# Beside the MLP, attention steps taken in twos: the order of one core's instructions rewritten for one stage of an attention-then-MLP kernel

## The chip, the core and the metric

The kernel runs on one core of a Trainium2 chip. A core has a matrix engine (PE, whose weight loads are shown as PEld), a vector engine (DVE), a scalar engine (ACT), a general engine (POOL) and a queue engine (SP) that issues most DMAs. Each takes its instructions in its own order and waits for the others through semaphores. Matrix products land in PSUM, eight banks of 128 x 512 float32. The metric is the device time of one execution in microseconds, lower is better.

## What is computed

```python
# q, k, v: 8 batches x 8 heads x 576 rows x 64; omega: 128 x 64
def phi(x):
    proj = np.einsum('bhsd,md->bhsm', x, omega)
    sq = np.sum(x * x, axis=-1, keepdims=True) / 2.0
    h = proj - sq
    h = h - np.max(h, axis=-1, keepdims=True)
    return np.exp(h) / np.sqrt(m)
q_p, k_p = (phi(q_s), phi(k_s))              # q_s, k_s: q and k scaled
kv = np.einsum('bhsm,bhsd->bhmd', k_p, v)
z = np.sum(k_p, axis=2)
num = np.einsum('bhsm,bhmd->bhsd', q_p, kv)
den = np.einsum('bhsm,bhm->bhs', q_p, z)[..., None] + 1e-06
x = (num / den)                              # then reshaped to 4608 x 512
g = x @ w_gate                               # 512 x 1536
out = (g * (1.0 / (1.0 + np.exp(-g))) * (x @ w_val)) @ w_out
```

All in float32. The MLP's products are made of three matmuls each, from a high and a low part of both operands (`hi`, `lo`).

## The kernel before

Attention works on groups of 256 rows of two heads: 72 groups of queries and 72 of keys. A step holds two groups: two of keys in the first six steps, then one of queries and one of keys, and two of queries in the last six (72 steps in all). A step goes through these functions, and they are what the order is made of:

- `st_transpose`: four PE transposes of the loaded rows (`nat`) into a bank `pt`, copied by ACT to `x`; POOL squares `nat` into `sq`.
- `st_project`: matmuls of `x` with `omT` into two banks `pp`. Each uses 64 of the array's 128 rows, and two run side by side. The profile shows 16 records for them, since a float32 matmul has two records.
- `st_max` (DVE: row sums of `sq`, maxima of both `pp`) and `st_exp` (ACT: eight exponentials from `pp` into `ph`).
- `k_accumulate`: matmuls of a key group's `ph` with `v` into the bank `kvacc`, two steps later. When a pair of heads is complete, `kv_finalize` copies `kvacc` to `kvr`, and for batches from 4 on transposes the row of sums (`zp`), copies it and sends it through DRAM (`zd`), from where `load_z` spreads it over all partitions (`zt`).
- the output of a query group in one of two ways. For batches 0 to 3: `q_transpose` (four transposes into `ptq`, copied by ACT to `qt`), `q_mult` (matmuls with `kvr` into `po`, divided on DVE into `xn`), then `q_out`, which transposes `xn` into `xt`. For batches 4 to 7 the divisor is made first (`q_den`: POOL product `jk`, DVE sum and reciprocal `dj`; `q_norm`: POOL scales `ph`), then `q_transpose`, and `q_out` multiplies `kvr` with `qt`, which gives the output already turned (`xt`, with 64 output columns per matmul). ACT then copies `xt` to `xo`, which is sent to DRAM for the last stage, or to `xh`, with DVE making `xl`.

PSUM is dealt out in pools: three banks for the MLP (`ps_moe`), two for projections (`ps_proj`), one bank `ps_att`, one bank `ps_tr`, and one for `kvacc`.

The kernel has three stages. Up to step 24 attention runs nearly alone (`CLOSE`). From step 25 (`EARLY`) on each step is one turn of the list `GROUPED`: its functions in turn, and between them six entries `SHARE`, at which the MLP stream is given its part of the work (`give`) and the conversion of the weights a few operations (`tick`). The MLP stream works through three tiles of 512 rows; per visit of a tile it makes three `g`, four `o` of the visit before, three `v`. When attention is done, the pools of attention are released, `first_x` prepares the operands of the last stage on DVE and ACT beside the last MLP work, and the last stage computes six tiles in pairs with seven products (`a`, `c`, `d`) in place of eight. It is not touched.

The order in the program is the order in which the functions are called, but a scheduler of the language may move an instruction ahead of others on its engine where its operands are there.

Of the kernel before, what the change touches and what calls it, by code (L numbers as in the profile page):

```python
# [24 lines left out]
def kernel(  # L25
# [16 lines left out]
    P = 128  # L42
# [387 lines left out]
    def st_transpose(n):  # L430
        if n >= NS:
            return
        nat = nats.pop(n)
        pt = ps_tr(f"pt_{n}", [P, 2, G])
        for i in range(2):
            for c in range(CH):
                turned_in[:] = [
                    transpose(
                        pt[:, i, c * P : (c + 1) * P], nat[:, i, c].rearrange("p h d -> p (h d)"), ident
                    )  # L440
                ]
        x = att.tile([P, 2, G], F32, name=f"x_{n}", tag="x")

        st = att.tile([P, 4, 2, CH, 2], F32, name=f"st_{n}", tag="st", bufs=6)
        sq = att.tile([P, 2, CH, 2, D], F32, name=f"sq_{n}", tag="sq")
        nc.gpsimd.tensor_tensor(sq, nat, nat, op=ALU.mult)  # L446
        if 3 <= n < EARLY:
            nc.scalar.copy(x[:, 0], pt[:, 0])
            nc.vector.tensor_copy(x[:, 1], pt[:, 1])
            for w in (D // 2, D // 4):  # L450
                lower_, upper_ = (sq[..., o : o + w].rearrange("p i c h d -> p (i c h) d") for o in (0, w))
                nc.gpsimd.tensor_tensor(lower_, lower_, upper_, op=ALU.add)
        else:
            nc.scalar.copy(x, pt)  # L454
        sts[n] = x, st, sq
        return True

    def st_project(n):
        if n >= NS:
            return  # L460
        x, st, sq = sts[n]

        new = ps_moe if n < EARLY and n % 2 else ps_proj
        pp = [new(f"pp{hh}_{n}", [P, 2, CH, M]) for hh in range(2)]
        for i in range(2):
            for c in range(CH):
# [51 lines left out]
    def kv_finalize(b, a2):  # L518
        acc = kvacc.pop((b, a2))
        raw = att.tile([P, 4, VW], F32, name=f"kvr{b}_{a2}", tag="kvr", bufs=4)  # L520
        nc.scalar.copy(raw, acc)  # L521
        for j in range(2):
            kvst[b, 2 * a2 + j] = raw[:, 2 * j : 2 * j + 2, :]
        if b >= BPOOL:

            zp = ps_att(f"zp{b}_{a2}", [4, P])
            transpose(zp, raw[:, :, D], ident)
            zs = att.tile([4, P], F32, name=f"zs{b}_{a2}", tag="zs")
# [5 lines left out]
    zds = {}  # L534
    zbc = {}

    def load_z(n):
# [12 lines left out]
    def q_den(n):  # L550

        n -= JLAG
        for _, b, g, gr in slots(n, "q"):
# [10 lines left out]
            else:  # L564
# [5 lines left out]
            dn = att.tile([P, 3, CH, 2], F32, name=f"dj{b}_{g}", tag="dj", bufs=6)  # L570
# [64 lines left out]
    def q_mult(n):  # L635

        n -= MLAG
        for _, b, g, gr in slots(n, "q"):
            if b >= BPOOL:
                continue  # L640
            qt = qts.pop((b, g))
            po = ps_att(f"po{b}_{g}", [P, CH, 2, VW])
            for c in range(CH):
                prs = pairs_of(gr)[c]
                w = P // len(prs) if gr is None else P
# [11 lines left out]
            xn = att.tile([P, CH, 2, D], F32, name=f"xn{b}_{g}", tag="jx")  # L657
            nc.vector.tensor_tensor(
                xn.rearrange("p c h d -> p (c h) d"),
                po[:, :, :, 0:D].rearrange("p c h d -> p (c h) d"),  # L660
# [10 lines left out]
    cols_done = [0]  # L671

    def q_out(n):
        n -= OLAG
        for i, b, g, gr in slots(n, "q"):
            po = (ps_att if n + OLAG < EARLY or i else ps_tr)(f"xt{b}_{g}", [P, G])
            first = column(b, gr)
            if b < BPOOL:
                xn = xns.pop((b, g))
                for c in range(CH):  # L680
                    transpose(po[:, c * P : (c + 1) * P], xn[:, c].rearrange("p h d -> p (h d)"), ident)
            else:
                qt = qts.pop((b, g))

                segs = [(pr, pr * RES, RES) for pr in range(NPAIR)] if gr is None else [(gr[0], 0, G)]
                for pr, o, w in segs:
                    for hh in range(2):
                        matmul(
                            po[hh * D : (hh + 1) * D, o : o + w], kvst[b, pr][:, hh, 0:D], qt[:, hh, o : o + w],
                            start=True, stop=True, skip_group_check=True,  # L690
                        )
            j, o = tile_of(first)
            if gr is None:
                parts_ = [(po.rearrange("d (r c) -> d r c", c=RES), slice(0, NPAIR), j, o, RES)]
# [18 lines left out]
        return bool(slots(n, "q"))  # L713


    def mm1(ps, wts, xs):
# [403 lines left out]
    def turn_next(n):  # L1120
# [11 lines left out]
        lambda n: k_accumulate(n, 1),  # L1132
        st_exp,
        q_den,
        lambda n: n == EARLY - 1 and q_out(n),
        lambda n: n == EARLY - 1 and q_mult(n),
    )
    GROUPED = (
        q_out,
        st_project,  # L1140
        q_transpose,
        lambda n: k_accumulate(n, 0),
        lambda n: k_accumulate(n, 1),
        st_max,
        st_exp,
        q_den,
        lambda n: st_transpose(n + 1),
        SHARE,
        SHARE,
        SHARE,  # L1150
        lambda n: q_norm(n + 1),
        q_mult,
        SHARE,
        SHARE,
        SHARE,
    )

    for n in range(2):
# [8 lines left out]
    warm(2, turned_in[0])  # L1167
    loaded = 3
    ends = []
    for n in range(NN):  # L1170
        if loaded <= n + LA:
            load(loaded)
            loaded += 1
# [3 lines left out]
            loaded += 1  # L1177
        if n == FIRST_RAW:
            load_raw(0)
        want = OPS * np.interp(clock[n + 1], [clock[m] for m, _ in marks], [x for _, x in marks])  # L1180
        order = CLOSE if n < EARLY else GROUPED
        left = len(order) if n < EARLY else order.count(SHARE)
        for what in order:
            with ExitStack() as es:
                if n < EARLY:
                    for ins in ends if what is st_project else ends[:1]:
                        es.enter_context(tc.issue_after(ins.ins))
                if what is not SHARE:
                    what(n)
            if n < EARLY:  # L1190
                if what is st_project:
                    ends.clear()
                ends.append(newest_pe[0])
            if what is turn_next and n < 2:
                warm(2, turned_in[0])
            if n < EARLY or what is SHARE:
                due = course[n + 1] - given[0] - debt[0]
                if due > 0:
                    give(due / left)
                for _ in range(int(np.ceil((want - ticks[0]) / left))):  # L1200
                    tick()
                left -= 1
        load_z(n)
    late.close()
    for name, pool in (
        ("win", tc.tile_pool(name="win", bufs=1)),
# [38 lines left out]
```

## Time and profile before

| | us |
|---|---|
| median of 3 runs | 1166.98 (1164.1 to 1167.11) |
| the profiled execution | 1166.82 |
| its span, first to last instruction | 1165.0 |
| first MLP matmul starts | 111 |
| last `xt` of attention starts | 562.7 |
| first product `a` of the last stage starts | 610.9 |

The profile is of one execution, so sums are made against 1166.82. Rows of groups give a line, an engine, the operation, tiles written and read, the shape, a count, the busy time and the mean of one in ns, then idle time ahead of it and what ended it. Rows in order of time give start, length, engine, line, operation and count; idle time ahead stands in brackets. Rows of stages give the stretch, its length, busy time and number of instructions of PE, PEld, DVE, ACT and POOL, the granted clock of PE, the DMA share and GB/s.

### The profile page before, as it was taken

Reading aid. Unit: us, or ns where it says so; the run is one execution under the profiler, and the core shown is the slowest. Engines: PE = TensorE matmul, PEld = TensorE weight load, DVE = VectorE, ACT = ScalarE, POOL = GpSimd, SP = SyncE. Lnnn points to the kernel's source line nnn. Section 1 sums busy time; section 2 is a strip of 40 time slices with the busy share of each in tenths; the row PEclk is TensorE's granted clock in tenths of the full one; section 3 lists DMA queues with packets and bytes.
Section 4 is the critical chain, followed back from the end, with each engine's and each line's share of the span. In section 5 each row is a group of like instructions: output and inputs, shape, how many; then the busy total and the mean of one; then the engine's idle time right before and its main releaser. Section 6 shows DMA issues by size and latency. Waiting matters only on the chain.

```text
span 1165.0 us, 18915 instructions
## 1 busy us (share of the span) xinstructions
PE 1137.2 (98%) x6645; PEld 939.5 (81%) x6646; DVE 707.4 (61%) x1289; ACT 678.3 (58%) x1539; POOL 615.5 (53%) x559
## 2 busy tenths in 40 slices
PE   8999999999999999989999999999999999999998
PEld 6888888888878778867788778888878888888886
DVE  5787667455656656565474566665566666456654
ACT  5887886876776866757434544454544445444441
POOL 5664433344556675587245555544455543455551
PEclk9999999999999999999999999999999999999999
DMA  6764445655445642322544111124211111211103
GB/s 137 179 160 114 128 142 161 178 135 143 122 126 137 168 132 78 114 68 65 154 118 126 46 55 55 55 74 122 59 55 55 54 37 46 81 55 55 46 19 72
DMA packets 173966, 114.30 MB, mean 98 GB/s; under 512 B 125840, under 2 KB 144304, under 8 KB 173872
## 3 DMA queue, kind: packets, MB, share of 16 engines
q1 hardware_dynamic: 172528, 112.78, 35.5%
q8 instruction: 52, 0.85, 0.3%
q10 hardware_dynamic: 1344, 0.33, 0.1%
q14 instruction: 42, 0.34, 0.1%
HBM read 87.88 MB, written 25.18 MB: 97 GB/s over the span
## 4 chain that ended last, share of the span: by engine, by line
PE 74%; DVE 10%; ACT 6%; POOL 4%; DMA 3%; issue 2%; SPq 1%; ACTq 0%; POOLq 0%; DVEq 0%
PE o L103 22%; PE a L103 16%; PE c L103 8%; PE g L103 6%; PE pp L103 4%; PE v L103 4%; PE d L103 4%; PE kvacc L103 3%; ACT ph L505 3%; PE ptq L107 2%; PE po L103 2%; PE pt L107 2%; PE xt L103 1%; DVE st L490 1%; POOL wlo L264 1%
## 5 line engine op out<-in xcount | busy, mean ns | idle before, releaser
L505 ACT ACTIVATE ph<-pp,st 128x128 f32<-128x128 f32 x576 | 157.8, 386 | 26.5 <-DVE st L493 26.0
L763 DVE TENSOR_TENSOR acc<-o,acc 128x512 f32<-128x512 f32 x156 | 105.8, 684 | 94.6 <-PE o L103 94.3
L446 POOL TENSOR_TENSOR sq<-nat 128x512 f32<-128x512 f32 x72 | 78.2, 1086 | 130.5 <-DVE st L483 89.1
L950 POOL TENSOR_TENSOR wlo<-wspare,whi 128x512 fp32r<-128x512 f32 (+1 forms) x60 | 61.0, 1037 | 117.4 <-ACT whi L949 111.0
L490 DVE TENSOR_REDUCE st<-pp 128x4 f32<-128x512 f32 x144 | 92.5, 683 | 39.0 <-PE pp L103 38.7
L264 POOL TENSOR_TENSOR wlo<-wraw,whi 128x512 fp32r<-128x512 f32 x59 | 82.7, 1406 | 26.7 <-ACT whi L263 22.8
L103 PE MATMUL pp<-omT,x 64*128 64x128 f32 x1152 | 87.3, 285 | 3.2 <-ACT x L454 2.2
L103 PEld LDWEIGHTS pp<-omT,x 64*128 64x128 f32 x1152 | 72.6, 187 | 20.2 <-issue 11.2
L950 POOL TENSOR_TENSOR wlo<-s,whi 128x512 fp32r<-128x512 f32 x64 | 82.6, 1311 | 3.8 <-ACT whi L949 3.8
L1059 ACT COPY late<-a 128x512 f32<-128x512 f32 x72 | 42.2, 586 | 59.7 <-PE a L103 58.5
L103 PE MATMUL o<-whi,late 128*128 128x512 f32 x192 | 74.5, 389 | 0.0
L571 DVE TENSOR_REDUCE dj<-jk 128x4 f32<-128x512 f32 x36 | 24.6, 684 | 73.5 <-POOL jk L567 60.6
L103 PE MATMUL kvacc<-v,ph 128*128 128x65 f32 x512 | 65.9, 268 | 0.5 <-ACT kvr L521 0.5
L824 POOL TENSOR_TENSOR hl<-sl,hh 128x512 fp32r<-128x512 f32 x36 | 47.0, 1308 | 34.8 <-ACT hh L823 34.7
L103 PEld LDWEIGHTS kvacc<-v,ph 128*128 128x128 f32 x512 | 63.1, 192 | 0.8 <-ACT kvr L521 0.6
L1063 DVE TENSOR_TENSOR late<-c,late 128x512 f32<-128x512 f32 x25 | 17.3, 692 | 69.7 <-PE c L103 60.6
L103 PE MATMUL g<-xh,whi 128*128 128x512 f32 x144 | 59.4, 412 | 0.0
L103 PE MATMUL o<-whi,hh 128*128 128x512 f32 x144 | 58.5, 406 | 0.1
L303 POOL TENSOR_TENSOR wc<-st 128x512 int32<-128x512 int32 x36 | 37.5, 1042 | 39.6 <-DVE st L298 17.2
L103 PE MATMUL v<-xh,whi 128*128 128x512 f32 x144 | 57.9, 402 | 0.0
L103 PE MATMUL g<-xh,wlo 128*128 128x512 f32 x144 | 57.7, 401 | 0.0
L103 PE MATMUL g<-xl,whi 128*128 128x512 f32 x144 | 57.2, 397 | 0.0
(261 smaller groups left out, 3369.4 us busy)
## 6 DMA issues: line engine op xcount, KB each, us to landing
wraw<-wscr SPq DMA_DIRECT2D x63, 256.0 KB, 2.7
wspare<-wscr SPq DMA_DIRECT2D x60, 256.0 KB, 2.8
wscr<-wc SPq DMA_DIRECT2D x36, 256.0 KB, 2.2
out_dram<-acc SPq DMA_DIRECT2D x72, 128.0 KB, 2.4
nat<-in_k_dram SPq DMA_DIRECT2D x64, 128.0 KB, 3.0
nat<-in_q_dram SPq DMA_DIRECT2D x64, 128.0 KB, 3.1
v<-in_v_dram SPq DMA_DIRECT2D x62, 128.0 KB, 3.5
st<-in_moe_w_gate_dram SPq DMA_DIRECT2D x12, 512.0 KB, 4.1
```

Of the source, the lines that this page charges most:

```text
L103: newest_pe[:] = [nc.tensor.matmul(*args, **kw)]
L107: newest_pe[:] = [nc.tensor.transpose(*args, **kw)]
L264: nc.gpsimd.tensor_tensor(lo, raw, hi.bitcast(F32), op=ALU.subtract)
L303: nc.gpsimd.tensor_tensor(ui, ri, low, op=ALU.add)
L446: nc.gpsimd.tensor_tensor(sq, nat, nat, op=ALU.mult)
L490: nc.vector.tensor_reduce(st[:, 1, :, :, hh], pp[hh], axis=AX.X, op=ALU.max, negate=True)
L505: step_end["s"] = nc.scalar.activation(ph[:, c, hh * M : (hh + 1) * M], pp[hh][:, i, c, :], AF.Exp, bias=st[:, 3, i, c, hh : hh + 1], scal ...
L571: nc.vector.tensor_reduce(dn[:, 0], jk, axis=AX.X, op=ALU.add)
L763: nc.vector.tensor_tensor(a_, po, a_, op=ALU.add)
L824: nc.gpsimd.tensor_tensor(hl, h, hh.bitcast(F32), op=ALU.subtract)
L950: nc.gpsimd.tensor_tensor(lo, src_, hi.bitcast(F32), op=ALU.subtract)
L1059: newest["s"] = nc.scalar.copy(keep[name], ps)
```

## The change

From step 25 on, one turn of a new list `DOUBLE` does two steps, n and n + 1 (24 turns with projections). Each entry names a function and which of the two steps it is for.

```diff
-        new = ps_moe if n < EARLY and n % 2 else ps_proj
-        pp = [new(f"pp{hh}_{n}", [P, 2, CH, M]) for hh in range(2)]
+        if n < EARLY:
+            new = (ps_moe, ps_moe) if n % 2 else (ps_proj, ps_proj)
+        else:
+            new = (ps_proj, ps_proj) if (n - EARLY) % 2 else (ps_att, ps_tr)
+        pp = [new[hh](f"pp{hh}_{n}", [P, 2, CH, M]) for hh in range(2)]
...
         if b >= BPOOL:
-            zp = ps_att(f"zp{b}_{a2}", [4, P])
+            zraw[b, a2] = raw
+    def z_rows():
+        for (b, a2), raw in zraw.items():
+            zp = ps_moe(f"zp{b}_{a2}", [4, P])
             transpose(zp, raw[:, :, D], ident)
...
-            po = ps_att(f"po{b}_{g}", [P, CH, 2, VW])
+            odd = n + MLAG >= EARLY and (n + MLAG - EARLY) % 2
+            po = (ps_tr if odd else ps_att)(f"po{b}_{g}", [P, CH, 2, VW])
...
+    def q_out_both(n):
+        groups = slots(n - 1 - OLAG, "q") + slots(n - OLAG, "q")
+        at = []
+        for k_, g_ in enumerate(groups):
+            if k_ % 2 == 0:
+                two = ps_moe(f"xt{g_[1]}_{g_[2]}", [P, 2, G])
+            at.append((g_, two[:, k_ % 2]))
+        place_out(at)
...
-    GROUPED = (
-        q_out,
-        st_project,
-        q_transpose,
-        lambda n: k_accumulate(n, 0),
-        lambda n: k_accumulate(n, 1),
-        st_max,
-        st_exp,
-        q_den,
-        lambda n: st_transpose(n + 1),
-        SHARE,
-        SHARE,
-        SHARE,
-        lambda n: q_norm(n + 1),
-        q_mult,
-        SHARE,
-        SHARE,
-        SHARE,
+    DOUBLE = (
+        (lambda n: k_accumulate(n, 0), 0),
+        (q_out_both, 0),
+        (st_project, 0),
+        (st_project, 1),
+        (lambda n: k_accumulate(n, 1), 0),
+        (q_norm, 0),
+        (st_max, 0),
+        (st_exp, 0),
+        (q_den, 0),
+        (st_max, 1),
+        SHARE,
+        SHARE,
+        SHARE,
+        (q_norm, 1),
+        SHARE,
+        SHARE,
+        SHARE,
+        (lambda n: z_rows(), 0),
+        (load_z, 0),
+        (load_z, 1),
+        (lambda n: k_accumulate(n, 0), 1),
+        (q_transpose, 0),
+        (st_transpose, 2),
+        (st_exp, 1),
+        SHARE,
+        SHARE,
+        (q_transpose, 1),
+        (st_transpose, 3),
+        (lambda n: k_accumulate(n, 1), 1),
+        SHARE,
+        SHARE,
+        (q_mult, 0),
+        (q_mult, 1),
+        SHARE,
+        SHARE,
+        (q_den, 1),
     )
...
+    for n in range(EARLY, NN, 2):
+        loads(n)
+        loads(n + 1)
+        left = DOUBLE.count(SHARE)
+        last = min(n + 2, NN)
+        for what in DOUBLE:
+            if what is not SHARE:
+                what[0](n + what[1])
+                continue
+            share(course[last] - given[0] - debt[0], wanted(last), left)
+            left -= 1
```

`place_out` is the body of the old `q_out`: it writes all groups' `xt` first and copies them afterwards. The buffers of `st` and `dj` go from six to four, `zs` from two to one, and `xn` gets a tag of its own, since it no longer fits beside `jk`'s. The last step of `CLOSE` no longer makes the output of step 24 and transposes the inputs of step 26 in place of it.

Three places on the engines' queues, as the programs hold them (the names are the tiles of the list above; `pp0_47` is step 47's projection of the first head).

PE, steps 47 and 48, the stretch with the projections. Before, step 47 alone; the matmuls left out are six more of `pp`, and MLP work follows the last row:

```order
L103 MATMUL xt4_2_4308<-qt4_2_4236,kvr4_1_3569 64x256 x2
L103 MATMUL pp0_47_4314<-omT_96,x_47_4268 128x128
L103 MATMUL pp1_47_4315<-omT_96,x_47_4268 128x128
...
L107 MATMUL ptq4_3_4324<-ident_90,ph0_45_4137 128x128 x4
L103 MATMUL kvacc5_1_4127<-v5_102,ph1_45_4142 128x65 x4
L107 MATMUL pt_48_4356<-ident_90,nat48_4088 128x128 x4
```

After, with six more of `pp` left out twice, between MLP matmuls on both sides:

```order
L103 MATMUL kvacc5_1_4126<-v5_102,ph1_45_4142 128x65 x2
L103 MATMUL xt4_1_4306<-qt4_1_4221,kvr4_0_3078 64x256 x2
L103 MATMUL xt4_1_4306<-qt4_2_4249,kvr4_1_3603 64x256 x2
L103 MATMUL pp0_47_4317<-omT_96,x_47_4228 128x128
L103 MATMUL pp1_47_4318<-omT_96,x_47_4228 128x128
...
L103 MATMUL pp0_48_4327<-omT_96,x_48_4256 128x128
L103 MATMUL pp1_48_4328<-omT_96,x_48_4256 128x128
...
L103 MATMUL kvacc5_1_4126<-v5_102,ph1_45_4142 128x65 x2
```

The two steps' outputs and projections stand in one stretch, and the transposes have left it. Counted over PE's order from step 25 to the last `xt`, stretches of `xt` matmuls and `pp` without other work between them go from 55 to 33, and stretches of MLP matmuls from 84 to 78.

ACT in the same turn, from the exponentials of step 47 to the copies of the second transposing group (`hh` is the MLP's, `st8` and `wc8` are the conversion's):

```order
L508 ACTIVATE ph1_47_4350<-pp1_47_4318,st_47_4229 128x128 x2
L301 ACTIVATE st8_0_3988<-st8_0_3988 128x512
L289 ACTIVATE wc8_1_4389<-st8_1_4191 128x512
L845 CAST hh4_4_4395<-sl4_4_4160 128x512
L643 COPY qt4_3_4420<-ptq4_3_4415 128x512
L454 COPY x_49_4427<-pt_49_4422 128x512
L508 ACTIVATE ph0_48_4432<-pp0_48_4327,st_48_4257 128x128 x2
```

Before, the same engine there (step 47's exponentials, then step 48's):

```order
L505 ACTIVATE ph1_47_4345<-pp1_47_4315,st_47_4269 128x128 x2
L301 ACTIVATE st8_0_4068<-st8_0_4068 128x512
L289 ACTIVATE wc8_1_4389<-st8_1_4196 128x512
L823 CAST hh4_4_4394<-sl4_4_4165 128x512
L703 COPY xo4_3_4_4418<-xt4_3_4415 128x256
L823 CAST hh4_5_4476<-sl4_5_4167 128x512
L633 COPY qt4_4_4436<-ptq4_4_4431 128x512
L454 COPY x_49_4468<-pt_49_4463 128x512
```

The copies of the transposes now stand between the exponentials of a pair's first and second step. On PE the transposes that they copy stand like this in the turn of steps 47 and 48; an MLP tile `g` follows:

```order
L107 MATMUL ptq4_3_4415<-ident_90,ph0_45_4137 128x128 x4
L107 MATMUL pt_49_4422<-ident_90,nat49_4085 128x128 x4
L103 MATMUL kvacc5_1_4126<-v6_103,ph1_46_4238 128x65 x2
L107 MATMUL ptq4_4_4443<-ident_90,ph0_46_4233 128x128 x4
L107 MATMUL pt_50_4450<-ident_90,nat50_4293 128x128 x4
```

In ten turns the two halves of this group stand together like this or with one or two MLP matmuls between them; in the others an MLP tile of 9 or 12 matmuls stands there. Between the projections and the first `ptq` stand 18 to 30 MLP matmuls, in five turns 12.

PE around the row of sums of batch 5 (`zp5_1`). Before, behind the accumulation that completes it:

```order
L107 MATMUL ptq4_5_4531<-ident_90,ph0_47_4340 128x128 x4
L103 MATMUL kvacc5_1_4127<-v7_104,ph1_47_4345 128x65 x4
L107 MATMUL pt_50_4571<-ident_90,nat50_4301 128x128 x4
L107 MATMUL zp5_1_4544<-ident_90,kvr5_1_4542 4x128
L103 MATMUL g5_5_4589<-xh2_1706,whi5_0_3210 128x512
```

After, where `kvacc5_1` was completed 12 MLP matmuls ahead of these rows:

```order
L103 MATMUL g5_5_4582<-xh2_1706,wlo5_0_3317 128x512
L107 MATMUL zp5_1_4598<-ident_90,kvr5_1_4545 4x128
L103 MATMUL kvacc6_0_4604<-v0_97,ph1_48_4437 128x65 x2
L107 MATMUL ptq4_5_4607<-ident_90,ph0_47_4345 128x128 x4
L107 MATMUL pt_51_4614<-ident_90,nat51_4300 128x128 x4
```

Behind the last `xt` of attention, 204 MLP matmuls stood ahead of the first product `a` of the last stage, and 180 stand there now.

More of the change, by code (lines that the diff above doesn't have):

```diff
@@ L442, in st_transpose @@
         x = att.tile([P, 2, G], F32, name=f"x_{n}", tag="x")
-        st = att.tile([P, 4, 2, CH, 2], F32, name=f"st_{n}", tag="st", bufs=6)
+        st = att.tile([P, 4, 2, CH, 2], F32, name=f"st_{n}", tag="st", bufs=4)
         sq = att.tile([P, 2, CH, 2, D], F32, name=f"sq_{n}", tag="sq")
@@ L524, in kv_finalize @@
         if b >= BPOOL:
-            zp = ps_att(f"zp{b}_{a2}", [4, P])
+            zraw[b, a2] = raw
+    zraw = {}
+    zds = {}
+    def z_rows():
+        for (b, a2), raw in zraw.items():
+            zp = ps_moe(f"zp{b}_{a2}", [4, P])
             transpose(zp, raw[:, :, D], ident)
-            zs = att.tile([4, P], F32, name=f"zs{b}_{a2}", tag="zs")
+            zs = att.tile([4, P], F32, name=f"zs{b}_{a2}", tag="zs", bufs=1)
             nc.scalar.copy(zs, zp)
@@ L532, in kv_finalize @@
             zds[b, a2] = zd
-    zds = {}
+        zraw.clear()
     zbc = {}
@@ L569, in q_den @@
                 )
-            dn = att.tile([P, 3, CH, 2], F32, name=f"dj{b}_{g}", tag="dj", bufs=6)
+            dn = att.tile([P, 3, CH, 2], F32, name=f"dj{b}_{g}", tag="dj", bufs=4)
             nc.vector.tensor_reduce(dn[:, 0], jk, axis=AX.X, op=ALU.add)
@@ L656, in q_mult @@
             nc.vector.reciprocal(dn[:, 1], dn[:, 0])
-            xn = att.tile([P, CH, 2, D], F32, name=f"xn{b}_{g}", tag="jx")
+            xn = att.tile([P, CH, 2, D], F32, name=f"xn{b}_{g}", tag="xn")
             nc.vector.tensor_tensor(
@@ L673, in q_out, with place_out @@
     def q_out(n):
-        n -= OLAG
-        for i, b, g, gr in slots(n, "q"):
-            po = (ps_att if n + OLAG < EARLY or i else ps_tr)(f"xt{b}_{g}", [P, G])
+        place_out([(g_, (ps_att if n < EARLY else ps_tr)(f"xt{g_[1]}_{g_[2]}", [P, G])) for g_ in slots(n - OLAG, "q")])
+    def q_out_both(n):
[6 more added lines that the diff above has]
+        place_out(at)
+    def place_out(at):
+        for (i, b, g, gr), po in at:
             first = column(b, gr)
@@ L691, in q_out @@
                         )
+        for (i, b, g, gr), po in at:
+            first = column(b, gr)
             j, o = tile_of(first)
@@ L712, in q_out @@
                 cols_done[0] = first + (RES if gr is None else G)
-        return bool(slots(n, "q"))
     def mm1(ps, wts, xs):
@@ L1134 @@
         q_den,
-        lambda n: n == EARLY - 1 and q_out(n),
         lambda n: n == EARLY - 1 and q_mult(n),
+        lambda n: n == EARLY - 1 and st_transpose(n + 2),
     )
-    GROUPED = (
-        q_out,
-        st_project,
-        q_transpose,
-        lambda n: k_accumulate(n, 0),
-        lambda n: k_accumulate(n, 1),
-        st_max,
-        st_exp,
-        q_den,
-        lambda n: st_transpose(n + 1),
+    DOUBLE = (
[9 more added lines that the diff above has]
+        (st_max, 1),
         SHARE,
@@ L1169, with loads @@
     ends = []
-    for n in range(NN):
+    def loads(n):
+        nonlocal loaded
         if loaded <= n + LA:
@@ L1179, with share, wanted @@
             load_raw(0)
[L1180 to L1183, printed above, removed]
-            with ExitStack() as es:
[L1185 to L1193, printed above, removed]
+    def share(due, want, left):
+        if due > 0:
+            give(due / left)
+        for _ in range(int(np.ceil((want - ticks[0]) / left))):
+            tick()
+    def wanted(n):
+        return OPS * np.interp(clock[n], [clock[m] for m, _ in marks], [x for _, x in marks])
+    for n in range(EARLY):
+        loads(n)
+        for at, what in enumerate(CLOSE):
+            with ExitStack() as es:
+                for ins in ends if what is st_project else ends[:1]:
+                    es.enter_context(tc.issue_after(ins.ins))
+                what(n)
+            if what is st_project:
+                ends.clear()
+            ends.append(newest_pe[0])
             if what is turn_next and n < 2:
                 warm(2, turned_in[0])
[L1196 to L1202, printed above, removed]
-        load_z(n)
+            share(course[n + 1] - given[0] - debt[0], wanted(n + 1), len(CLOSE) - at)
+        load_z(n)
+    for n in range(EARLY, NN, 2):
+        loads(n)
+        loads(n + 1)
[7 more added lines that the diff above has]
+            left -= 1
     late.close()
```

## The prediction

> **What bounds the kernel now.** I read the page first, then the sums by stage, then the waits of PE alone.
>
> ```profile
> span 1165.0 us, 18915 instructions
> PE 1137.2 (98%) x6645; PEld 939.5 (81%) x6646; DVE 707.4 (61%) x1289; ACT 678.3 (58%) x1539; POOL 615.5 (53%) x559
> ...
> 147.00:380.00 233.00, 229.77 (x1600) 191.58 (x1599) 137.99 (x300) 169.88 (x407) 113.72 (x99) 1.00 0.52 142
> 380.00:512.00 132.00, 128.68 (x874) 102.56 (x872) 78.00 (x164) 92.70 (x232) 86.81 (x78) 0.99 0.44 121
> 512.00:560.00 48.00, 42.33 (x264) 31.43 (x265) 28.14 (x54) 31.09 (x77) 35.78 (x33) 1.00 0.21 60
> ```
>
> PE is busy for 98% of the span and no other engine passes 61%. The change touches the stage in which attention steps run beside the MLP, about 147 to 565 us. There PE is still busy for 229.77 of 233 us and 128.68 of 132; only in the last 48 us, where the keys are used up and two query groups are done per step, does it stand still for 5.7. So this stage gets shorter in two ways only: PE work that costs less, or fewer waits of PE. The waits of PE from 147 to 610 us (total, times, longest):
>
> ```profile
> PE ptq L107 <- ACT xo L703: 2.9, 4, 2.1
> PE xt L107 <- DVE xn L658: 2.3, 2, 1.2
> PE zp L107 <- ACT kvr L521: 2.0, 3, 1.1
> PE pt L107 <- ACT qt L633: 1.9, 1, 1.9
> PE pp L103 <- ACT ph L505: 1.0, 2, 0.8
> PE pt L107 <- ACT xo L703: 0.7, 2, 0.4
> PE xt L103 <- ACT x L454: 0.7, 1, 0.7
> ```
>
> They sum to 11.5 us: all that could ever be won from waiting, 1% of the kernel. The rest must come from how PE's own instructions follow each other. One attention step there, PE in order of time:
>
> ```profile
> 457.81 0.28 PE L103 MATMUL pp<-omT,x 64*128 64x128 f32 x2
> 458.02 0.66 PE L107 MATMUL ptq<-ident,ph 128*128 128x128 f32 x4
> ...
> 464.82 0.39 PE L103 MATMUL v<-xl,whi 128*128 128x512 f32 x1
> 465.05 0.39 PE L103 MATMUL v<-xh,wlo 128*128 128x512 f32 x1
> 465.37 0.65 PE L103 MATMUL xt<-qt,kvr 128*64 128x256 f32 x4
> 465.95 1.16 PE L103 MATMUL pp<-omT,x 64*128 64x128 f32 x16
> 467.04 0.66 PE L107 MATMUL ptq<-ident,ph 128*128 128x128 f32 x4
> 467.54 1.00 PE L103 MATMUL kvacc<-vrest,ph 128*128 128x65 f32 x8
> 468.38 0.61 PE L107 MATMUL pt<-ident,nat 128*128 128x128 f32 x4
> ```
>
> Ends are modelled, so I read starts. No row has idle time, yet it is not all at full pace. MLP matmuls start 0.23 apart, but the last one before `xt` (64 output columns) takes 0.32: entering the half-size shapes costs 0.09. The 16 records of `pp` (64 rows, two at a time) take 1.09; the last pair, before the full-size `ptq`, takes 0.21, so the other seven take 0.126 each: leaving costs 0.085.
>
> **The change, part by part.** All sums are against the profiled execution, 1166.82 us (1.8 more than its span, 0.2 under the median of the runs shown).
>
> (1) Fewer entries and exits. In PE's order from step 25 to the last `xt`, the stretches of half-size matmuls fall from 55 to 33, with the same matmuls in them. 22 x (0.09 + 0.085) = 3.9 us. In the second half, where the output is made by `xt` matmuls, two groups now follow each other:
>
> ```profile
> 547.52 1.08 PE L103 MATMUL xt<-qt,kvr 128*64 128x256 f32 x8
> ...
> 548.53 0.50 PE L103 MATMUL v<-xh,whi 128*128 128x512 f32 x1
> ```
>
> Eight records take 1.01 us; two stretches of four take 2 x 0.58 = 1.16. That is 0.15 for each of 13 pairs of steps, 2.0 us. Together -5.9, with 3.9 and 7.2 (0.15 at all 22) as ends. Stretches of MLP work fall from 84 to 78; I give that nothing. Splitting `kvacc` into halves costs nothing: its records run at 0.1 either way.
>
> The Trainium skill (TensorEngine Tiling, Key Properties) says that a change of the tiling mode drains the TensorE, and TensorE: Matmul & The Clock Gate, step 4 of Part 2, puts a drain at about 128 cycles, 53 ns at 2.4 GHz. Three changes for each of 22 stretches would be 3.5 us by that estimate, and the sum 2.4 us less of a gain; the rows show more per change than the page.
>
> (2) `zp` transposes. They stood right behind the last `kvacc`, waiting for ACT's copy: 2.0 us above. One such wait also cost clock:
>
> ```profile
> 424.75 0.27 PE L107 MATMUL zp<-ident,kvr 128*4 128x128 f32 x1 [1.14 <-ACT kvr L521]
> ...
> 425.85 0.63 PE L103 MATMUL g<-xh,whi 128*128 128x512 f32 x1
> 426.28 0.63 PE L103 MATMUL g<-xl,whi 128*128 128x512 f32 x1
> ...
> 425.80:429.20 3.40, 3.40 (x10) 2.46 (x8) 1.77 (x4) 3.11 (x10) 2.37 (x3) 0.59 0.55 131
> ```
>
> At a granted clock of 0.59, seven matmuls start 0.43 apart in place of 0.23: 1.4 us. Now `zp` comes after at least 12 MLP matmuls, 2.7 us against a longest wait of 1.1. -3.4 (end: 0, if ACT is as late there). The `zd` writes and `zt` reads move with it on SP's queue; the product that needs them is half a turn away. The loads of two steps are now issued together at the start of a turn:
>
> ```profile
> nat<-in_q_dram SPq DMA_DIRECT2D x64, 128.0 KB, 3.1
> ```
>
> The later of the two transposes that need them stands some 8 us behind (its turn's first stretch and most of its MLP shares), against 3.1 to land, and the buffers they go to were read a turn before. I cost this at nothing; it would cost what is missing of the 3.1 if the transposing group stood at the turn's start.
>
> (3) `pp` behind `ph`, 1.0 us: the second projection of a pair uses banks last read a whole turn earlier. -1.0.
>
> (4) `ptq` and `pt` behind ACT's `xo` copy, 2.9 + 0.7: they shared a bank with `xt`, which moves to the MLP's three. The same copy now frees an MLP bank, and I give 1.5 back. -2.1 (ends 0 and -3.6). The waits behind `qt`, `xn` and `x` I leave as they are: the new order still has each of them, at like distances.
>
> (5) New waits, not in this trace. The first projection of a pair now lies in the two banks that its query transposes and the next `pt` want. PE takes its instructions in order, so `ptq`, and the MLP matmuls queued behind it, wait until DVE has taken the maxima and ACT all eight exponentials. One such chain:
>
> ```profile
> 233.50 1.21 DVE st L490 x2
> ...
> 234.74 0.18 DVE st L492
> ...
> 234.94 0.18 DVE st L493
> ...
> 235.40 0.95 ACT ph L505 x4
> ...
> 236.40 0.91 ACT ph L505 x3
> ```
>
> From 233.50 to 237.31 is 3.8 us. Over it lie the second projection (8 x 0.126 = 1.0), two halves of `kvacc` (0.4 each) and the MLP between: 24 matmuls (5.5) in most pairs, 12 (2.7) in five. Cover is 4.5 in the worst, 7.3 in most. In those five I put 0.5 each for an engine that is still busy when the chain starts: 2.5. In the second transpose group, ten pairs have no MLP tile between the first `ptq`, `pt` and the second:
>
> ```profile
> L633 ACT COPY qt<-ptq 128x512 f32<-128x512 f32 x72 | 42.5, 599 | 23.3 <-PE ptq L107 23.3
> ...
> L454 ACT COPY x<-pt 128x512 f32<-128x512 f32 x50 | 29.8, 596 | 18.6 <-PE pt L107 18.2
> ```
>
> There PE reaches the second `pt` 1.8 us after the first `ptq` starts (0.5 + 0.4 + 0.4 + 0.5 for `ptq`, `pt`, half a `kvacc`, `ptq`), while its bank comes free after the 0.66 of that `ptq` and ACT's two copies of 0.6 (`qt`, then `x`), with hand-overs of some 0.05 about 2.0: 0.2 each, 2. For the seam at step 25, 0.5. +5, with 0 and 24 x 0.73 = 17.5 (the mean of the four `xo` waits above, in every pair) as ends; I stay near the low one because most pairs have 3 us to spare.
>
> (6) The hand-over to the last stage. The pieces of its chain, in order of time:
>
> ```profile
> 599.77 0.61 DVE acc L763
> ...
> 600.42 2.34 PE o L103 x9
> ...
> 610.92 1.36 PE a L103 x6
> ```
>
> DVE's preparation runs until 599.77 and delays an `o` by next to nothing; the first product `a` starts 11 us later. In the new order 24 fewer MLP matmuls (5.4 us) lie between the last attention output and that product. The products keep 5 us of slack, but `o` and `v` tiles now queue behind DVE sooner, though two of their `acc` adds move ahead of its last pieces. +1, ends 0 and 5.4.
>
> Sum: -5.9 - 3.4 - 1.0 - 2.1 + 5 + 1 = -6.4, so 1160.4 us.
>
> **Rivals.**
>
> *The banks become the bound.* Were DVE or ACT regularly 3 us late when the projection ends, every pair would wait for its exponentials. At 0.73 for 24 pairs this costs 17.5: 1166.8 - 12.4 + 17.5 + 1 = 1172.9. It beats all gains from 0.48 a pair on, and makes the kernel visibly slower from 0.62. For it: two maxima now follow each other on DVE, and both engines are 58 to 61% busy. Against it: 24 matmuls of cover in most pairs. 0.17.
>
> *The gains are paid back.* New waits of 0.45 a pair, 10.8 us: 1166.8 - 12.4 + 10.8 + 1 = 1166.2. For it: the order has 24 pairs with two new places to wait in each (the first `ptq`, the second `pt`), and the waits behind `xn` and `qt`, 2.3 and 1.9 us above, are still there. Against it: most pairs have 3 us to spare at the first place and the second is worth 0.2. 0.23.
>
> *The clock drops.* A drop costs about 1.4 us above; one in each pair gives 24 x 1.4 = 34, 1194 after the other terms. The new transposing stretch of 2.2 us is longer than any before.
>
> ```profile
> 25.00:50.00 25.00, 24.00 (x250) 22.29 (x251) 17.40 (x46) 18.98 (x63) 14.65 (x20) 1.00 0.79 186
> ```
>
> Against it: here PE does attention alone and the clock is 1.00; the one drop followed 1.4 us of idle PE. 0.02. The Trainium skill (TensorE: Matmul & The Clock Gate, Part 4) says that transposes do not count as PE-busy in the same way for the clock; this rule would favour the drop, and the trace bears it out in no stretch without idle time.
>
> That the order doesn't change as it says is no rival: it stands above.
>
> **How the numbers follow.** A measurement of this kernel tells about 0.3% from no change, 3.5 us. The forecast has 0.58 and ends at 1160.4; paid back 0.23 at 1166; slower cases 0.17 and 0.02. So faster 0.58, same 0.23, slower 0.19. Without any new wait it would be 1166.8 - 12.4 = 1154.4, and with a little more from (1) 1153; on the other side the bank rival's 1172.9 is nearly all taken in by 1172. Range 1153 to 1172.
>
> **What would show it.** (1): `xt` followed by 32 `pp` records in about 2.1 us, then `kvacc`. (2): no PE wait behind `kvr`, no stretch at 0.59. (5): waits of `ptq` or `pt` behind `ph`, `qt` or `x` of 5 us in all; over 12 and the forecast is wrong. (6): PE idle within 10 us before the first `a`. It is wrong, too, if MLP tiles wait behind `xo`, since (4) took that as small.

## The result, and the profile after

| | before | after |
|---|---|---|
| median, us | 1166.7 (1164.1 to 1167.11, 4 runs) | 1181.92 (1180.98 to 1183.97, 4 runs) |
| the profiled execution | 1166.82 | 1181.06 |
| its span | 1165.0 | 1179.3 |
| last `xt` of attention ends | 563.8 | 580.7 |
| first product `a` starts | 610.8 | 625.0 |
| mean granted clock of PE | 0.997 | 0.992 |

The changed kernel takes 1.0138 times as long, with an interval of [1.0116, 1.0159]. It is slower by 15 us where 6 us less were forecast. The head of the profile's page:

```profile
span 1179.3 us, 18916 instructions
...
PE 1138.2 (97%) x6646; PEld 951.9 (81%) x6646; DVE 707.4 (60%) x1289; ACT 668.7 (57%) x1535; POOL 616.0 (52%) x559
```

PE, DVE and POOL are as busy as before to within 1 us, and ACT 10 us less (four loads of its function table are gone, and they took 1.28 each); the span has grown by 14.3 us in which PE stands still or runs slowly. They lie ahead of the first `a`: from there to the end the two kernels take 554.3 and 554.2 us. The waits of PE from 25 to 660 us (what waits, for which engine and tile, total, times, longest):

```profile
PE po L103 <- ACT qt L643: 6.4, 4, 3.1
PE ptq L107 <- ACT qt L643: 5.8, 5, 2.5
PE pt L107 <- ACT qt L643: 2.2, 1, 2.2
PE g L103 <- DVE sl L842: 2.2, 1, 2.2
PE pt L107 <- ACT x L454: 2.2, 2, 1.2
PE o L103 <- ACT sl L822: 1.9, 2, 1.4
PE xt L103 <- ACT qt L643: 1.7, 1, 1.7
...
PE v L103 <- ACT sl L822: 1.1, 1, 1.1
...
PE kvacc L103 <- ACT kvr L524: 0.8, 2, 0.5
PE ptq L107 <- ACT ph L508: 0.6, 1, 0.6
```

The waits of `zp` behind `kvr`, of `pp` behind `ph` and of `ptq` and `pt` behind `xo` are gone, as forecast. In their place stand 16.1 us behind ACT's copy `qt` and 2.2 behind its copy `x`. The exponentials `ph`, for which the prediction had set aside 2.5, hold PE up once, for 0.6. New as well are waits of the MLP's own tiles behind DVE's and ACT's operations on `sl`: up to the last `xt` three of them, 3.8 us in all, where the kernel before has none.

Who waits for whom has turned round. The same two groups of ACT copies from 107 to 581 us, which is step 24 to the last `xt`, before and then after (count, busy time and mean; last, ACT's idle time ahead of them and what ended it):

```profile
L633 ACT COPY qt<-ptq 128x512 f32<-128x512 f32 x55 | 31.9, 591 | 21.2 <-PE ptq L107 21.2
L454 ACT COPY x<-pt 128x512 f32<-128x512 f32 x47 | 28.0, 595 | 16.6 <-PE pt L107 16.2
```

```profile
L643 ACT COPY qt<-ptq 128x512 f32<-128x512 f32 x55 | 32.6, 604 | 5.3 <-PE ptq L107 5.3
L454 ACT COPY x<-pt 128x512 f32<-128x512 f32 x47 | 29.2, 622 | 1.4 <-PE pt L107 1.4
```

Before, ACT stood ready at these copies and waited 37.8 us for PE's transposes. After, it waits 6.7, though it has no more work: it comes to them late. One of the long stalls shows how. PE, then ACT, then POOL of the changed kernel in order of time (start, length, instruction, count; idle time ahead and its end in brackets):

```profile
290.50 0.60 PE L107 MATMUL ptq<-ident,ph 128*128 128x128 f32 x4
290.93 0.60 PE L107 MATMUL pt<-ident,nat 128*128 128x128 f32 x4
291.37 0.56 PE L103 MATMUL kvacc<-v,ph 128*128 128x65 f32 x4
295.03 2.67 PE L103 MATMUL po<-kvr,qt 128*128 128x65 f32 x16 [3.11 <-ACT qt L643]
297.45 0.77 PE L103 MATMUL v<-xh,whi 128*128 128x512 f32 x1
298.03 0.63 PE L103 MATMUL v<-xl,whi 128*128 128x512 f32 x1
298.45 0.63 PE L103 MATMUL v<-xh,wlo 128*128 128x512 f32 x1
```

```profile
289.72 1.16 ACT L263 CAST whi<-wraw 128x512 fp32r<-128x512 f32 x2
293.84 0.67 ACT L289 ACTIVATE wc<-st 128x512 f32<-128x512 f32 x1 [2.96 <-POOL wlo L264]
294.41 0.57 ACT L643 COPY qt<-ptq 128x512 f32<-128x512 f32 x1
```

```profile
292.55 2.50 POOL L264 TENSOR_TENSOR wlo<-wraw,whi 128x512 fp32r<-128x512 f32 x2
```

`ptq` is there by 291.1, but its copy stands in ACT's queue behind a step of the weight conversion (L289), which waits for the first of POOL's two operations to release a tile and starts at 293.84. The copy runs at 294.41. `po` wants the bank `ps_att`, in which `ptq` lies; its own operand is another `qt`, made long before. The MLP matmuls queued behind `po` wait with it. Then PE runs at part clock: the `v` matmuls start 0.42 and more apart in place of 0.23.

A balance from step 24's projection (at 107.13 and 107.20 us) to the end of the last `xt`. PE idle is the sum of PE's gaps over 0.1 us there; the rest is the total less idle time and less 0.227 for each MLP matmul (their distance at full clock), that is attention matmuls, changes of shape and low clock. The last column is the time at a granted clock of 0.50.

| | total | MLP matmuls in it | PE idle | rest | at half clock |
|---|---|---|---|---|---|
| before | 456.7 | 1056 | 12.1 | 204.9 | 3.4 |
| after | 473.5 | 1080 | 23.5 | 204.8 | 17.1 |
| difference | +16.9 | +5.4 us | +11.5 | 0.0 | +13.7 |

From the last `xt` to `a` the 24 matmuls are saved again, but it takes only 2.7 us less (47.0, 44.3). Half clock stands in four places after (from 156.2, 296.2, 524.9 and 545.3 us) and in one before (from 425.2). PE is busy for 16.6 and 3.4 us in them; work that takes twice as long there costs half of that, 8.3 and 1.7, a difference of 6.6. So the rest holds a gain of 6.6 that the clock took back.

### The profile page after: what moved, and what is told of

It is laid out like the page before. It is cut to its first block, busy times and chain, and to the rows that moved or that the text cites. A ratio compares the mean times of both kernels' runs of the same rounds, so it can differ in the third digit from the quotient of the medians.

```text
span 1179.3 us, 18916 instructions
## 1 busy us (share of the span) xinstructions
PE 1138.2 (97%) x6646; PEld 951.9 (81%) x6646; DVE 707.4 (60%) x1289; ACT 668.7 (57%) x1535; POOL 616.0 (52%) x559
## 4 chain that ended last, share of the span: by engine, by line
PE 64%; DVE 6%; ACT 5%; POOL 3%; issue 2%; DMA 2%; SPq 0%; POOLq 0%; ACTq 0%; DVEq 0%
PE o L103 21%; PE a L103 16%; PE c L103 8%; PE v L103 4%; PE g L103 4%; PE d L103 4%; PE pp L103 2%; ACT ph L508 2%; PE kvacc L103 2%; PE xt L103 1%; PE ptq L107 1%; PE po L103 1%; PE pt L107 1%; POOL jk L577 1%; POOL wlo L264 1%
## 5 line engine op out<-in xcount | busy, mean ns | idle before, releaser
L508 ACT ACTIVATE ph<-pp,st 128x128 f32<-128x128 f32 x576 | 160.1, 393 | 27.7 <-DVE st L496 27.3
L264 POOL TENSOR_TENSOR wlo<-wraw,whi 128x512 fp32r<-128x512 f32 x59 | 82.9, 1410 | 18.9 <-ACT whi L263 18.7
L103 PE MATMUL pp<-omT,x 64*128 64x128 f32 x1152 | 83.5, 281 | 2.1 <-ACT x L454 2.1
L103 PEld LDWEIGHTS kvacc<-v,ph 128*128 128x128 f32 x512 | 68.3, 191 | 6.6 <-ACT kvr L524 1.0
L103 PE MATMUL kvacc<-v,ph 128*128 128x65 f32 x512 | 72.1, 268 | 0.5 <-ACT kvr L524 0.5
L846 POOL TENSOR_TENSOR hl<-sl,hh 128x512 fp32r<-128x512 f32 x36 | 47.0, 1312 | 45.2 <-ACT hh L845 44.3
L103 PE MATMUL o<-whi,hl 128*128 128x512 f32 x144 | 56.8, 395 | 0.0
```

Source lines behind the costliest of these rows:

```text
L103: newest_pe[:] = [nc.tensor.matmul(*args, **kw)]
L264: nc.gpsimd.tensor_tensor(lo, raw, hi.bitcast(F32), op=ALU.subtract)
L508: step_end["s"] = nc.scalar.activation(ph[:, c, hh * M : (hh + 1) * M], pp[hh][:, i, c, :], AF.Exp, bias=st[:, 3, i, c, hh : hh + 1], scal ...
L846: nc.gpsimd.tensor_tensor(hl, h, hh.bitcast(F32), op=ALU.subtract)
```

## The experiments

Eighteen runs, each timed beside the kernel before. Times are medians.

### The conversion left out, in both kernels (e1, e2)

```diff
             u = moe.tile([P, DM], F32, name=f"wc{f}_{i}", tag="wraw", bufs=3)
-            (two ACT, three DVE operations, POOL's add)
+            nc.gpsimd.memset(u, 0.0)
...
```

> The changed kernel, in which the weights are not rebuilt from their two halves: of each piece the two ACT operations, the three of DVE and POOL's add are left out (POOL fills the tile with zeros, the loads and stores stay), so the MLP's values are others. Theory A (lateness: the second transposes and po wait because ACT's qt copy stands in its queue behind conversion work that itself waits): with that work gone PE's waits behind qt, x and ph fall from 17 us to under 5, the clock drops go, and the time is 0 to 6 us below that of the kernel before without conversion. Rival B (distance: second ptq, pt and po follow the first ptq by too few matmuls whatever else ACT does): those waits stay at 10 us or more, and the time is 8 us or more above that of the kernel before without conversion.

> The kernel before with the same work left out. Theory A: PE's waits fall a little (12 to about 6 us), since they were spread; the time falls by 3 to 10 us, and lies 0 to 6 us above the changed kernel without conversion. Rival B: it lies 8 us or more below the changed kernel without conversion.

Changed 1157.68, before 1155.31. Against the kernel before in full these are 0.9934 [0.9919, 0.9949] and 0.9915 [0.9898, 0.9932]. Of the 15 us that the changed kernel loses, about 2.4 are left (the intervals overlap a little). PE idle in the stretch of the table is 11.5 and 5.4 us. The waits of the changed kernel that concern us, first, and of the kernel before:

```profile
PE pt L107 <- ACT x L438: 3.3, 1, 3.3
PE ptq L107 <- ACT qt L627: 2.6, 3, 1.0
...
PE pt L107 <- ACT qt L627: 2.0, 1, 2.0
```

```profile
PE ptq L107 <- ACT xo L687: 2.3, 2, 2.1
PE pt L107 <- ACT qt L617: 1.9, 1, 1.9
```

Neither theory holds as written. Most of the loss needs the conversion (A), but waits behind `qt`, `x` and `ph` fall only from 18.9 to 9.5 and not under 5. The longest of them, `pt` behind `x`, ends after this on ACT:

```profile
289.88 2.17 ACT L492 ACTIVATE ph<-pp,st 128x128 f32<-128x128 f32 x8 [1.43 <-DVE st L480]
292.07 1.28 ACT L806 ACT_TABLE_LOAD   x1
293.36 1.08 ACT L806 ACTIVATE sl<-g 128x512 f32<-128x512 f32 x2
294.33 0.59 ACT L438 COPY x<-pt 128x512 f32<-128x512 f32 x1
```

Late maxima, the exponentials, a table load and `silu` stand ahead of the copy: ACT is late without the conversion too, only less often.

### po in other banks, and one more share between the groups (e3, e4, e9)

```diff
-            odd = n + MLAG >= EARLY and (n + MLAG - EARLY) % 2
-            po = (ps_tr if odd else ps_att)(f"po{b}_{g}", [P, CH, 2, VW])
+            po = (ps_proj if n + MLAG >= EARLY else ps_att)(f"po{b}_{g}", [P, CH, 2, VW])
```

e4 has this too, and two shares instead of three behind `q_norm` of the second step, three instead of two between the transposing groups. e9 has only the shares.

> The changed kernel with po (the products of q_mult) in the two projection banks, which are free by then, instead of in the banks of the transposes. The po that waited behind an unrelated qt copy (6.4 us in 4 places) no longer does. Theory A and B alike: these 6 us go, and with them two or three stretches at half clock (1.6 us each), so 1172 to 1176. Rival C (the wait only moves: the next instruction, an MLP tile or a pt behind the same ACT queue, takes it over): less than 2 us gained, 1180 to 1182.

> As e3, and one of the MLP shares that stood ahead of the first transposing group stands between the two groups, so that nearly every pair has a tile of 12 matmuls (2.7 us) there. Rival B: the second ptq and pt lose their waits (8 us), 1164 to 1169. Theory A: lateness of 2 to 4 us is longer than one tile, about half of it goes, 1168 to 1173. Rival D (the first group now comes too soon after the projection and waits for the exponentials): no gain over e3 or a loss, with waits of ptq behind ph.

> The changed kernel with the shares spread as in e4, po left in the banks of the transposes. From e4 against e3 (4.4 us) the spread is worth 4 us: 1177 to 1178 if the two parts add up. If po's waits behind an unrelated qt grow because fewer shares stand between the second transposes and q_mult in time (none is taken away there), little is gained: 1180 to 1182. If the first group had been what po's bank waited for, the spread alone does most of the work: 1170 or less.

e3 1171.8 (1.0038 [1.002, 1.0055]), e4 1167.37 (1.0016 [1.0005, 1.0026]), e9 1184.41 (1.0151 [1.0135, 1.0166]). po's wait for a bank with whose contents it has nothing to do was worth 10 us by the medians; in the profiles of the two PE idle falls by 4.6 (23.5 to 18.9) and the rest by 3.5 (to 201.3). The shares win 4 us on top of that and nothing alone, where `po` still waits 5.7 behind `qt` and 27.3 us pass at half clock (17.1 in the changed kernel). So the parts don't add up.

### The reserve of MLP work for the hand-over (e5)

```diff
-    MARGIN = 45.0
+    MARGIN = 50.5
```

> The changed kernel with the planner's reserve (MARGIN) at 50.5 instead of 45, so that 1056 MLP matmuls stand ahead of the last xt and 204 between it and the first product a, as before the change (1080 and 180 in the changed kernel). Theory H (the smaller reserve costs the 2.3 us that o and v wait there): those waits go and the time falls by 2 to 3 us, to 1179 to 1180. Rival (the waits there cover something that must be done anyway, or the tiles taken out of the pairs were cover for them): no gain, 1181 to 1184.

1188.41 (1.0188 [1.0175, 1.0201]): 6.5 us slower than the changed kernel. From the last `xt` to `a` it takes 49.0 us for 204 matmuls, 2.7 more than 204 x 0.227; the changed kernel's 44.3 for 180 are 3.4 more, and the kernel before's 47.0 for 204 are 0.7 more. So the wait at the hand-over doesn't come from the smaller reserve. With fewer matmuls in the turns of two steps, PE idle ahead of the last `xt` rises from 23.5 to 27.4 us and the time at half clock from 17.1 to 27.3; that the matmuls taken out had been cover is the likely reading, not shown by itself.

### The conversion moved within a turn (e7, e10)

Its steps (`tick`) are issued only at the first two and the last four shares of a turn; otherwise e4. e10 has e5's reserve as well.

```diff
+    NO_TURN = (2, 3, 4, 5, 6, 7)
...
+        if not turns:
+            return
```

> As e4 (po in other banks, shares spread; 1167.4), and the steps of the weight conversion are issued at the first two and the last four MLP shares of a pair only, so that none of them is issued between the last of the maxima and the second transposes; as many as before in all. Theory A (lateness): the waits of ptq, pt and kvacc behind qt, x and kvr, 12 us in e4, fall to 6 or less; 1160 to 1164. Rival E (the lateness comes from silu, hh, the landing weights and table loads, as in the run without conversion, where 6 us of them stayed): less than 2 us gained, 1165 to 1168. Rival F (the conversion now stands ahead of xo and the next exponentials): waits of xt or of the first ptq, 1168 or more.

> e7 and e5 together: po in other banks, shares spread, conversion out of the middle of a pair, reserve as before the change. If all parts add up, 1157 to 1161, faster than the kernel before (1165.9). If the conversion wasn't the cause and the reserve is worth 2.5, 1163 to 1165. If neither holds, 1167.

e7 1165.54 (0.9991 [0.9978, 1.0004]), no different from the kernel before; e10 1174.7 (1.0079 [1.0067, 1.0091]). In e7 waits behind `qt` remain (9.2 of `pt` and `ptq`): rival E, since e4 itself was 1167.4. Again the larger reserve costs, 9 us here.

### Other engines for the copies, or for one step of the conversion (e11, e12, e13, e15)

```diff
-            nc.scalar.copy(qts[b, g], pt)
+            (nc.scalar.copy if m < EARLY else nc.vector.tensor_copy)(qts[b, g], pt)
```

is e11. e12 (changed kernel), e13 (before) and e15 (e7) have instead

```diff
-                nc.scalar.activation(u, r, AF.Abs)
+                nc.vector.scalar_tensor_tensor(u, r, -1.0, r, op0=ALU.mult, op1=ALU.max)
```

> The changed kernel with the qt copy of all query transposes beside the MLP on DVE instead of ACT. Theory A in its narrow form (what matters is that qt stands in ACT's queue behind conversion, silu and landing weights): the waits of po, ptq, pt and xt behind qt (16 us of 23.5) go, and with them the stretches at half clock (5 us): 1163 to 1170. Rival G (DVE is as late as ACT, with the maxima, the acc additions and its own conversion steps in its queue): the same waits appear behind a qt copy of DVE, 1178 to 1186. In between, 1170 to 1178, both engines are late, at different places.

> The changed kernel with the first step of the weight conversion (the absolute value, which waits on ACT for POOL to release its tile: 2.6 to 3.0 us at three places) on DVE instead of ACT. If ACT's waiting at that step is what delays qt: two to four of the long stalls go, 1171 to 1177. If the landing weights, silu and table loads are enough, 1179 to 1183. If DVE now waits there ahead of the maxima and the exponentials come late: 1184 or more, with waits of ptq behind ph.

> The kernel before with the same step on DVE. The control: if the step matters only where the transposes lie close together, 1164 to 1168, as the kernel before.

> As e7 (po in other banks, shares spread, conversion out of the middle of a pair; 1165.5), and the absolute value on DVE. If what is left in e7 (waits behind qt of 9 us) came from ACT's waiting conversion step: 1158 to 1162, faster than the kernel before. If it came from silu, landing weights and table loads: 1164 to 1167.

e11 1196.09 (1.0264 [1.0247, 1.0281]), slower than anything else and 10 us past rival G's range too. The narrow form of theory A falls: DVE is late too, and `pt` now waits 8.9 us behind ACT's copy `x`, where it waited 2.2. In e11 its queue and then PE show the same picture as above, with the copy behind a conversion step that waits for ACT's:

```profile
290.39 0.79 DVE L292 TENSOR_SCALAR wc<-wc 128x512 f32<-128x512 f32 x1 [3.83 <-ACT wc L289]
291.10 0.68 DVE L643 COPY qt<-ptq 128x512 f32<-128x512 f32 x1
```

```profile
291.83 1.54 PE L103 MATMUL po<-kvr,qt 128*128 128x65 f32 x6 [3.83 <-DVE qt L643]
```

e12 1176.58, with a wide interval (1.01 [1.0066, 1.0134]): inside what was expected if that step on ACT matters, but one wait of 5.2 us behind `qt` has come in its profile. e13 1167.41 (1.0017 [1.0008, 1.0026]): the kernel before hardly notices. e15 1171.85 (1.0053 [1.0038, 1.0068]), 6 us above e7 where 1158 to 1167 was expected; `xt` now waits 6.4 us behind DVE's `xn`. Moving the load between ACT and DVE moves the place of the wait.

### The distance of the transposing groups (e19, e18, e16, e17)

All with `po` as in e3, and these numbers of shares: ahead of the first transposes, between them and the second, behind those.

| | ahead, between, behind | median | ratio |
|---|---|---|---|
| e19 | 6, 0, 6 | 1180.7 | 1.011 [1.0089, 1.0131] |
| e3 | 6, 2, 4 | 1171.8 | 1.0038 [1.002, 1.0055] |
| e4 | 5, 3, 4 | 1167.37 | 1.0016 [1.0005, 1.0026] |
| e18 | 5, 4, 3 | 1179.41 | 1.0106 [1.0079, 1.0132] |
| e16 | 4, 5, 3 | 1178.61 | 1.0101 [1.0082, 1.0119] |
| e17 | 3, 6, 3 | 1176.31 | 1.0079 [1.0064, 1.0094] |

In e16 to e18 `q_mult` stands between the groups, in the others behind them.

> As e3 (1171.8, two shares between the transposing groups), with no MLP share between the two groups, six ahead of the first and four behind the second. Theory B (distance): every second ptq and pt waits for ACT's two copies and whatever stands before them, 1180 or more. Rival (pairing itself, or the exponentials ahead of the first group): the longer cover ahead of the first group helps, 1165 to 1172.

> As e3, with five shares ahead of the first group, four between the two (po's products among them, ahead of the second transposes) and three behind. Theory B: 1162 to 1166. Rival: 1167 to 1172.

> As e18 with four shares ahead and five between. Theory B: 1160 to 1165, waits behind qt and x below 5 us. Rival: 1167 to 1172, waits of the first ptq behind ph as it now comes sooner after the projection.

> As e18 with three shares ahead and six between, the distance that the groups had before. Theory B: 1158 to 1164, unless the three shares ahead no longer hide the maxima and exponentials: then waits of the first ptq behind ph of 5 us or more and 1165 to 1170. Rival: 1167 to 1172.

In e16 to e18 two things change at once, so these runs don't test distance alone. With no share between, `ptq` waits behind `qt` ten times (e19); with four, not once, but `po` in its new banks now waits for the exponentials (e18):

```profile
PE ptq L107 <- ACT qt L643: 12.4, 10, 3.6
```

```profile
PE po L103 <- ACT ph L508: 9.1, 6, 4.1
PE pt L107 <- ACT qt L643: 4.7, 2, 2.4
PE xt L103 <- ACT qt L643: 3.9, 3, 1.8
```

So distance does what theory B says at its own place, and not for the time: PE idle is 25.0, 24.3, 23.8 and 23.6 us in e19, e18, e16 and e17, against 16.7 in e4. Both theory and rival missed the times from four shares on. The waits say why: a share that is moved ahead of one bank's next use is missing ahead of another's.

### Late engines, and too few free banks (e21, e20)

e21 is e4 without the conversion. e20 is the kernel before with `MARGIN` 50.5.

> e4 (po in the projection banks, shares spread) with the work of the weight conversion left out as in e1 and e2. Lateness met by too few free banks: the waits fall below those of e1 (11.5 us) to 6 to 8, the gain from fewer switches (5.4 us there) shows, and the time is 1150 to 1154, below the kernel before without conversion (1155.3). If pairing costs waits whatever the other engines do: 1156 to 1160.

> The kernel before with the planner's reserve at 50.5 instead of 45: 1032 MLP matmuls ahead of the last xt instead of 1056. If its order has room for lateness wherever the tiles lie: 1165 to 1169. If it is as sensitive as the changed kernel (6.5 us from the same step): 1171 or more, and part of the difference between the two kernels is only how their tiles happen to meet ACT's late stretches.

e21 1149.5 (0.9862 [0.9845, 0.9878]), 5.8 us below the kernel before without conversion (0.9915 [0.9898, 0.9932]); the intervals lie apart. PE idle in the stretch is 7.0 us. With `po` in other banks, shares spread and less work on the engines that copy, the paired order does win about what its prediction said (6.4):

```profile
PE pt L107 <- ACT qt L627: 3.5, 2, 2.1
PE po L103 <- DVE xl L716: 1.9, 4, 0.7
```

e20 1167.56 (1.0012 [1.0003, 1.0022]): the kernel before loses 1 or 2 us from the step that costs the changed one 6.5. Its order has room for late engines; that of the changed kernel has not.

## Why the prediction was wrong, point by point

(1) Fewer entries and exits, -5.9: right. The two outputs and two projections in one stretch run as forecast, 32 records of `pp` in 2.0 us:

```profile
493.91 1.08 PE L103 MATMUL xt<-qt,kvr 128*64 128x256 f32 x8
494.92 2.06 PE L103 MATMUL pp<-omT,x 64*128 64x128 f32 x32
496.91 0.66 PE L103 MATMUL kvacc<-v,ph 128*128 128x65 f32 x4
```

By the balance (rest 0.0, clock 6.6) it is -6.6 in the changed kernel. The same sum, the rest less its low clock, gives -10.7 in e7 (195.7 - 3.2 against 204.9 - 1.7) and -11.7 in e21 against e2 (191.3 - 1.7 against 201.3). So the sign and the rows hold and the size is rather too small; which changes of shape the rest saves beyond the two counted isn't shown.

(2) `zp`, -3.4: the wait of 2.0 is gone; the 1.4 for low clock is not won, since the clock drops in four other places, to 0.50.

(3) `pp` behind `ph`, -1.0: gone, as said.

(4) `ptq` and `pt` behind `xo`, -2.1: all 3.6 are gone, and no MLP tile waits behind `xo`. The 1.5 given back for the MLP bank that `xt` now takes stands against 3.8 of waits of MLP tiles behind `sl`; whether they come from that bank isn't shown. The same paragraph holds the sentence that failed: "The waits behind `qt`, `xn` and `x` I leave as they are: the new order still has each of them, at like distances." The sentence fails in two ways. The second `ptq` is no longer at a like distance: it now follows within a tile of 12 MLP matmuls, or none, the `ptq` whose bank it takes; before, a step lay between. `po` is at a like distance in most turns: it took the bank of its step's `ptq` before too, mostly 9 to 18 MLP matmuls behind it, and once none, without a wait:

```profile
250.84 0.66 PE L107 MATMUL ptq<-ident,ph 128*128 128x128 f32 x4
...
252.61 1.00 PE L103 MATMUL po<-kvr,qt 128*128 128x65 f32 x8
```

Now it stands 9 to 16 behind in six turns of ten and at most 3 in four, and one of its two long waits (2.42, ahead of 156.05) comes 13 behind. There the distance is the old one, and what is new is that the copy comes late.

(5) New waits, +5: the term that decided. It looked for them behind the exponentials (2.5, measured 0.6) and, in the second group, at 0.2 for each of ten pairs, from the length of two copies on an ACT that starts at once. Measured: 18.9 us behind `qt`, `x` and `ph`, of which 6.4 at `po`, which the prediction didn't list at all. The rows that it quoted for the length of these copies also had ACT's idle time ahead of them, 23.3 and 18.6 us: room to be late, which the new order takes away. Low clock after the waits, 6.6, was no term of the sum.

(6) The hand-over, +1: measured +2.7. Its reason, 24 fewer matmuls, fell with e5. What else puts it off was not tried.

With what was measured: -6.6 (1), +11.5 PE idle (with the waits of (2) to (4) that went), +6.6 clock, +2.7 (6) make +14.2 of the 14.3 us. Among the rivals, "the banks become the bound" named the kind of mechanism, and the slower side, but with the wrong engine work (exponentials) and at 1172.9. "The clock drops" had one drop in each pair; there are four in all. The test it set itself, `ptq` and `pt` behind `ph`, `qt` or `x` over 12 us, reads 10.8 and would have passed for lack of `po`.

What stays open: which waiting operation makes ACT late in each case (conversion, `silu` with its table load, landing weights) could be shown for single stalls, not priced one by one; and why the same step of `MARGIN` adds 6.5 and 9 us in e5 and e10 is seen only as more and other waits (PE idle +3.9 and +6.7) and more low clock (+4.3 and +3.9, by half of PE's busy time in it). No version that does all the work is faster than the kernel before by more than the measurement tells.

## What to carry to other kernels

Where an edit brings the next user of a bank closer to the copy that frees it, or makes that copy later, don't compare lengths: read the idle time ahead of that copy on its engine. If the copying engine waits for PE there, it has been early, and that idle time is the allowance which the edit spends; then list what may stand ahead of the copy in its queue and wait itself. To tell lateness from distance, take work off the late engines in both kernels alike and compare those two.

## What the runs showed of the hardware

Low clock follows a pause of PE, but not by the pause's length alone. Here are two pauses of 2.42 us each, ahead of 156.05 us in the changed kernel and, second fence, ahead of 524.46 in e18. The granted clock is the third figure from the right, PE's busy time the third from the left (behind the stretch and its length):

```profile
152.80:156.21 3.41, 0.98 (x5) 0.52 (x4) 1.25 (x3) 3.41 (x11) 1.27 (x1) 1.00 0.79 236
156.21:159.62 3.41, 3.41 (x17) 3.41 (x18) 1.06 (x4) 3.38 (x6) 2.28 (x2) 0.50 0.44 100
```

```profile
519.22:522.63 3.41, 2.82 (x17) 2.08 (x15) 3.41 (x8) 2.40 (x9) 1.93 (x2) 1.00 0.18 58
522.63:526.04 3.41, 1.58 (x9) 1.42 (x10) 0.25 (x3) 1.77 (x4) 3.35 (x4) 1.00 0.00 0
526.04:529.46 3.42, 3.42 (x33) 2.26 (x34) 2.61 (x4) 2.12 (x3) 3.42 (x3) 1.00 0.01 4
```

The rows are cut where the granted clock can change: in each of the twenty traces all its changes lie on one grid of slots of 3.41 us, which starts elsewhere in each execution. The first pause lies within one slot, with PE busy for 0.98 us of it, and half clock follows. The second is split between two slots, busy for 2.82 and 1.58, and no half clock follows. In the twenty traces, without their first 5 us, 6722 slots ran at full clock. All 71 with PE busy for less than 46% were followed by half clock, and none of the 6566 above 64%; of the 85 between them 16 were (busy as this profile models it). In the prediction's rows a pause of 1.14 us was followed by 0.59: its slot, from 421.78 to 425.20, has PE busy for 1.99. So what a pause costs is in part luck, since it hangs on where the grid lies. The four executions of e12, one program, took 1182.87, 1178.24, 1174.92 and 1173.08 us at mean granted clocks of 0.987, 0.991, 0.995 and 0.997.

The Trainium skill (TensorE: Matmul & The Clock Gate, Why this matters for your kernels) asks for no idle gaps over some 3 us between bursts of matmuls. The pauses above that agree: half clock came with all 19 of them in the twenty traces. But shorter ones cost clock as well, and which of them do isn't told by their length. So a wait of PE can cost more than its idle time: 6.6 us of low clock came with 11.5 of waits here.
